# Transposing the operands of attention by DMA rather than on TensorE, in a fused attention and mixture kernel

## Chip, cores, metric

One core of a Trainium2 chip. The metric is the time of one execution on the device in microseconds (us). Profiles are of one execution each. Their "span" runs from the first to the last instruction. Most executions of a kernel agree within some tenths of a per cent. A run is called slow when it is over 1.5% above the fastest of the same kernel.

Engine names in the profile: PE is TensorE (PEld its weight loads), DVE is VectorE, ACT is ScalarE, POOL is GpSimd, SP the engine that here only issues DMAs.

## The reference, cut

```python
# attention: batch 4, 8 heads, 768 steps, head dimension 48
f = 1.0 / (1.0 + np.exp(-f_logit))
for t in range(S):
    state = f[:, :, t, :, None] * state + np.einsum('bhd,bhe->bhde', k[:, :, t], v[:, :, t])
    y[:, :, t] = np.einsum('bhd,bhde->bhe', q[:, :, t], state)
# mixture: 3072 tokens, d_model 384, d_ff 2048, x is y laid out by tokens
h = x @ w_in
P = a[0] + a[1] * h + a[2] * h * h + a[3] * h * h * h
Q = 1.0 + np.abs(b[0]) * np.abs(h) + np.abs(b[1]) * h * h
out = (P / (Q + 1e-06)) @ w_out
```

The work is cut into 12 units of 256 tokens (0 to 11). Attention of a unit runs chunk by chunk; its output is projected to 2048 columns in two groups of 8 x 256, on which P/Q is computed, and projected back.

## The kernel before

The order of all work is a fixed list of tokens, key and unit: `mq`/`mk` are the VectorE products that write q and k scaled (tile `qkp`), `T` transposes them, `Te` copies the result out of PSUM (tile `qkT`), `sc` are the scores that read it. In the mixture, `t` and `B` are two affine functions of y, `P` adds them, `U` adds |y| and its square, `O` copies out and stores.

```python
P_BY_DMA = {4, 5, 6, 7, 8, 9, 10, 11, 12, 13, 14, 15, 16, 17, 18, 19, 20, 21}
...
def a_T(n, ps=ALL):                                  # 16 blocks of 128x128 on PE
    ...
                nc.tensor.transpose(tp[:, b, i, p, :],
                                    s["qk"][:, i, ps.start + p, b].rearrange("t i d -> t (i d)"), ident)
def a_Te(n, ps=ALL):                                 # PSUM -> SBUF, on ACT or VectorE
    ...
        copy(te_engine(n), t.rearrange("p j a b c -> p (j a b c)"), ...)
...
def m_t(n):                                          # per group of 2048 columns
    nc.vector.tensor_scalar(tile_of(n, "t", bufs=3), mg[n]["y"], a_sb[:, 3:4], a_sb[:, 2:3],
                            op0=ALU.mult, op1=ALU.add)
def m_p(n):                                          # the last sum of the numerator
    if n in P_BY_DMA:
        nc.gpsimd.dma_start(out=s["t"], in_=s["pb"], accum_op=ALU.add)
    else:
        nc.vector.tensor_add(s["t"], s["t"], s["pb"])
...
def m_oe(m, b, eng, queue=None):
    osb = ms.tile([P, DM], F32, name="osb", bufs=4)
    copy(eng, osb, ops.pop((m, b)))
    ...
    (queue or nc.sync).dma_start(out=dst[:, b, :], in_=osb)        # stores: SP queue
...
# load(n): f, k and q of unit n, 384 KB each, also on the SP queue
```

Of the kernel before, what the change touches and what calls it, by code (L numbers as in the profile page):

```python
# [18 lines left out]
    efl-:0 efl:0 cs-:0 A0-:0 A1-:0 cs:0 A1:0 mk-:0 A0:0 mq-:0 T-:0 mk:0 mq:0 Te-:0 T:0 sc0:0 sv:0 Te:0  # L19
    efl:1 m0:0 al:0 sc1:0 st:0 cs:1 A0:1 m1:0 y-:0 mq:1 y:0 A1:1 mk:1 sw:0 su:0 xe:0 T:1 Te:1 ha0:0  # L20
    Ya0:0 ha1:0 sc0:1 sv:1 m0:1 Ya1:0 vl:3 al:1 st:1 sc1:1 za:0 efl:2 qa:0 cs:2 A1:2 ta:0 Ua:0 m1:1 sa:0
    hb0:0 sw:1 Ba:0 y:1 mk:2 A0:2 hb1:0 La0:0 Pa:0 Yb0:0 Ea:0 su:1 xe:1 mq:2 Yb1:0 T:2 ga:0 ha1:1 Te:2
    Ya1:1 ha0:1 zb:0 qb:0 Ya0:1 tb:0 Ub:0 Lb0:0 sc0:2 m0:2 Bb:0 hb0:1 sv:2 Ba:1 sc1:2 hb1:1 al:2 za:1
    m1:2 oa0:0 st:2 sw:2 Yb0:1 Eb:0 y:2 Yb1:1 qa:1 efl:3 sb:0 cs:3 xe:2 tb:1 A1:3 ta:1 Pb:0 ha1:2 A0:3
    zb:1 Ya1:2 gb:0 mq:3 ha0:2 Ya0:2 su:2 efl:4 qb:1 Bb:1 hb1:2 Yb1:2 oa1:0 Ua:1 Oa:0 cs:4 mk:3 T:3 Ub:1
    ta:2 La0:1 ob0:0 ob1:0 sa:1 sv:3 vl:4 Te:3 A1:4 sc0:3 qa:2 Ea:1 Ob:0 A0:4 efl:5 hb0:2 mk:4 m0:3
    sc1:3 mq:4 al:3 vl:5 m1:3 cs:5 st:3 sw:3 Lb0:1 sb:1 A0:5 y:3 za:2 Yb0:2 Pb:1 ua1:2 A1:5 qb:2 xe:3
    Eb:1 ua0:2 La1:2 su:3 T:4 sv:4 Pa:1 zb:2 La0:2 ga:1 Ub:2 ha0:3 Te:4 Ba:2 al:4 ha1:3 sc0:4 tb:2 mk:5
    gb:1 m0:4 Ya0:3 sa:2 efl:6 st:4 mq:5 vl:6 oa0:1 Bb:2 Ya1:3 Ea:2 oa1:1 sc1:4 hb1:3 sb:2 m1:4 sw:4
    Yb1:3 hb0:3 Oa:1 cs:6 Yb0:3 ob0:1 A0:6 y:4 za:3 qb:3 Pa:2 A1:6 ob1:1 qa:3 Lb0:2 ta:3 xe:4 su:4 T:5  # L30
    ha0:4 sa:3 zb:3 sv:5 Pb:2 Ba:3 ha1:4 ga:2 tb:3 Eb:2 Bb:3 Te:5 Ob:1 sc0:5 oa0:2 Ya0:4 efl:7 Ua:3 gb:2
    m0:5 mq:6 Ub:3 al:5 Pa:3 st:5 Ya1:4 oa1:2 Oa:2 hb0:4 sc1:5 La0:3 mk:6 Yb0:4 ob0:2 Ea:3 sw:5 sb:3
    vl:7 m1:5 hb1:4 ta:4 Yb1:4 cs:7 Lb0:3 qa:4 za:4 y:5 Ua:4 ob1:2 Ba:4 xe:5 T:6 sa:4 qb:4 zb:4 A1:7
    ha1:5 A0:7 su:5 sv:6 mq:7 Te:6 sc0:6 Pb:3 Ya1:5 Ob:2 ga:3 m0:6 Ub:4 ha0:5 sc1:6 al:6 st:6 Eb:3 oa0:3
    La0:4 hb0:5 Ya0:5 tb:4 m1:6 y:6 Ea:4 Pa:4 vl:8 sb:4 Bb:4 gb:3 za:5 sw:6 xe:6 mk:7 qa:5 oa1:3 Yb0:5
    Oa:3 hb1:5 ta:5 su:6 Ba:5 sa:5 T:7 Te:7 sv:7 ha1:6 efl:8 Yb1:5 ga:4 al:7 Lb0:4 Ya1:6 tb:5 cs:8 A0:8
    sc0:7 ob0:3 st:7 ob1:3 m0:7 zb:5 A1:8 ua1:5 sc1:7 Pb:4 sw:7 qb:5 m1:7 Eb:4 La1:5 ha0:6 gb:4 Ya0:6
    ua0:5 Ob:3 y:7 hb1:6 mq:8 efl:9 Bb:5 sb:5 mk:8 La0:5 xe:7 Pa:5 cs:9 Yb1:6 A0:9 T:8 Ub:5 ta:6 za:6
    oa0:4 Ea:5 Ba:6 qa:6 su:7 hb0:6 oa1:4 Te:8 A1:9 Yb0:6 ha1:7 sa:6 Lb0:5 ga:5 vl:9 ha0:7 Ya1:7 Oa:4
    sc0:8 Pb:5 tb:6 zb:6 sv:8 qb:6 ob0:4 m0:8 Pa:6 ua1:6 Ya0:7 al:8 Eb:5 mk:9 ua0:6 La1:6 st:8 La0:6  # L40
    sc1:8 ob1:4 sb:6 Bb:6 m1:8 Ba:7 za:7 sv:9 Ub:6 efl:10 hb0:7 Ea:6 y:8 hb1:7 Yb0:7 xe:8 gb:5 mq:9 Pb:6
    ha0:8 vl:10 Ob:4 qa:7 al:9 T:9 ta:7 Ua:7 Yb1:7 st:9 Bb:7 Lb0:6 ha1:8 Ya0:8 oa0:5 qb:7 Ya1:8 Te:9
    zb:7 oa1:5 Eb:6 Oa:5 cs:10 efl:11 ga:6 A0:10 A1:10 sa:7 sc0:9 Pa:7 hb0:8 tb:7 ob0:5 m0:9 sc1:9 gb:6
    ta:8 Yb0:8 mq:10 m1:9 ob1:5 hb1:8 La0:7 ub1:7 Ba:8 mk:10 qa:8 Yb1:8 y:9 Ob:5 za:8 Ea:7 Lb1:7 sb:7
    xe:9 vl:11 ga:7 ub0:7 tb:8 Lb0:7 Ua:8 zb:8 oa0:6 qb:8 cs:11 A1:11 T:10 A0:11 Pb:7 Te:10 Eb:7 Ub:8
    oa1:6 ha1:9 Oa:6 sa:8 sv:10 sc0:10 al:10 ha0:9 La0:8 st:10 mk:11 m0:10 Ya1:9 ob0:6 Ya0:9 Ea:8 ob1:6
    sc1:10 Pa:8 Lb0:8 sb:8 hb1:9 Bb:8 Ob:6 m1:10 hb0:9 Yb0:9 za:9 qa:9 sv:11 y:10 gb:7 ta:9 Yb1:9 xe:10
    mq:11 Ba:9 Eb:8 oa0:7 qb:9 Pb:8 al:11 T:11 Ua:9 zb:9 sa:9 Te:11 oa1:7 ga:8 ha0:10 Oa:7 sc0:11 tb:9
    La0:9 Ub:9 ha1:10 st:11 ob0:7 m0:11 sc1:11 Ya1:10 Ya0:10 Pa:9 Bb:9 ob1:7 Ea:9 sb:9 m1:11 hb0:10 Ob:7
    Lb0:9 hb1:10 za:10 qa:10 y:11 gb:8 Pb:9 Ua:10 Yb0:10 oa0:8 oa1:8 ta:10 Yb1:10 Ba:10 xe:11 Eb:9 Oa:8  # L50
    La0:10 sa:10 ha0:11 ha1:11 zb:10 qb:10 ob0:8 ga:9 Pa:10 Ub:10 tb:10 ob1:8 Bb:10 Ya0:11 sb:10 Ya1:11
    Pb:10 Ea:10 gb:9 za:11 hb1:11 Ob:8 Yb1:11 hb0:11 qa:11 Yb0:11 ta:11 Ba:11 oa0:9 sa:11 Ua:11 Lb0:10
    oa1:9 qb:11 zb:11 Oa:9 ob0:9 ga:10 tb:11 Ub:11 Eb:10 La0:11 ob1:9 Ea:11 Pa:11 Ob:9 gb:10 Lb0:11
    ob0:10 oa0:10 sb:11 Bb:11 ob1:10 Eb:11 ga:11 oa1:10 Oa:10 oa0:11 Pb:11 ob0:11 gb:11 ob1:11 oa1:11
    Oa:11 Ob:10 Ob:11
# [3 lines left out]
P_BY_DMA = {4, 5, 6, 7, 8, 9, 10, 11, 12, 13, 14, 15, 16, 17, 18, 19, 20, 21}  # L59

U_BY_DMA = {2, 3, 5, 6, 7, 8, 9, 11, 13, 14, 16, 17, 18, 19, 20, 21, 22, 23}

TE_ON_ACT = {1, 2, 4, 5, 6, 11}
O_ON_DVE = {(0, 1), (11, 1), (10, 1), (2, 0), (9, 1)}
# [3 lines left out]
def kernel(  # L68
# [12 lines left out]
    nc = tc.nc  # L81
# [61 lines left out]
    hold = w_pool.tile([1, 4, 16], BF16, name="hold")  # L143
# [6 lines left out]
    NUN = len(units)  # L150
    at_ = {}
# [3 lines left out]
    def load(n):  # L155
        c, u = units[n]
        at_[n] = dict(qk=qkp[n % NQK], ls=lsp[n % NQK], st=states[u], c=c, u=u)
        for name, src in (("fn", f_logit), ("kn", k), ("qn", q)):
            at_[n][name] = ld.tile([C, H, UB, D], F32, name=name)
            if n > 0:  # L160
                nc.sync.dma_start(out=at_[n][name].rearrange("p h b d -> p h (b d)"), in_=rows(src, n))
        if n == 0:
            for ps in HALVES:
                for name, src in (("fn", f_logit), ("kn", k), ("qn", q)):
                    for i in range(2):
                        hs = slice(HP * i + ps.start, HP * i + ps.stop)
                        nc.sync.dma_start(out=at_[n][name][:, hs].rearrange("t h b d -> t h (b d)"),
                                          in_=rows(src, n)[:, hs])

    def load_v(n):  # L170
        at_[n]["vn"] = vz[n % NV]
        for cc in range(UB):
            w = slice(CH * cc, CH * cc + CH)
            nc.gpsimd.dma_start(out=vz[n % NV][w, :, cc].rearrange("p h b d -> p h (b d)"), in_=rows(v, n)[w])  # L174

# [59 lines left out]
    def a_T(n, ps=ALL):  # L235

        s = at_[n]
        pool, tag = (psr, "r") if ps is HALVES[1] else (psA, "A")
        tp = pool.tile([P, UB, 2, npairs(ps), C], BF16, name="tp", tag=tag)
        for b in range(UB):  # L240
            for i in range(2):
                for p in range(npairs(ps)):
                    nc.tensor.transpose(tp[:, b, i, p, :],  # L243
                                        s["qk"][:, i, ps.start + p, b].rearrange("t i d -> t (i d)"),
                                        ident)
        s["tp", ps.start] = tp

# [3 lines left out]
    def a_Te(n, ps=ALL):  # L251
        s = at_[n]
        t = tile_at(s, "qkT", [P, UB, 2, HP, C], BF16)
        if ps is ALL:
            copy(te_engine(n), t.rearrange("p j a b c -> p (j a b c)"),
                 s["tp", 0].rearrange("p j a b c -> p (j a b c)"))
        else:
            copy(te_engine(n), t[:, :, :, ps].rearrange("p j a b c -> p (j a) (b c)"),
                 s["tp", ps.start].rearrange("p j a b c -> p (j a) (b c)"))
# [29 lines left out]
    def a_sc(n, half):  # L289
# [3 lines left out]
        for q_ in range(2):  # L293
            p = half * 2 + q_
            for b in range(UB):
                for i in range(2):
                    for cc in range(UB):
                        r, w = slice(64 * i, 64 * i + D), slice(CH * cc, CH * cc + CH)
                        nc.tensor.matmul(sc[w, i, q_, b, :], s["qkT"][r, b, 1, p, w], qcols(s, r, p, w),  # L299
# [7 lines left out]
    def qcols(s, r, p, w):  # L307
        return s["qkT"][r, :, 0, p, w]
# [10 lines left out]
    def a_y(n, ps=ALL):  # L319
# [7 lines left out]
        def clear(kk, r):  # L327
# [28 lines left out]
        if ps.start == 0:  # L356
            for kk in (0, KD - 1):
                clear(kk, slice(0, P))
        product(True, [(1, 1)])
        product(False, [(1, 1)])  # L360
        for i in range(2):
            if ps.start == 0:
                clear(0, slice(64 * i + 32, 64 * i + 48))
            if ps.stop == HP:
                clear(KD - 1, slice(64 * i, 64 * i + 16))
# [46 lines left out]

    def m_y(n, half):
        nc.scalar.copy(part_of(tile_of(n, "y"), half), mg[n]["hp", half].rearrange("p a n -> p (a n)"))  # L414

    def m_sq(n):
        s = mg[n]
        s["h2"] = ms.tile([P, W], BF16, name="h2")
        nc.vector.tensor_mul(s["h2"], s["y"], s["y"])  # L419

    def m_abs(n):
        s = mg[n]
        s["z"] = ms.tile([P, W], BF16, name="z")
        nc.vector.tensor_scalar(s["z"].bitcast(U16), s["y"].bitcast(U16), 0x7FFF, None,  # L424
# [21 lines left out]
    def m_ln(n, half):  # L446
        s = mg[n]
        lq = tile_of(n, "lq", F32, bufs=1)
        whole = "u" in s
        nc.scalar.activation(lq if whole else part_of(lq, half),  # L450
                             s["u"] if whole else s["u", half].rearrange("p a n -> p (a n)"),
                             AF.Ln, scale=sig[:, 2:3], bias=1.0 + 1e-6)
# [5 lines left out]

    def m_t(n):
        nc.vector.tensor_scalar(tile_of(n, "t", bufs=3), mg[n]["y"], a_sb[:, 3:4], a_sb[:, 2:3],  # L460
# [210 lines left out]
```

## Time and profile before

| | before |
|---|---|
| time, median of the first 3 runs | 234.65 us (233.94 to 234.94) |
| span of the profiled execution | 231.3 us |
| busy: PE, VectorE, ACT | 211.0, 212.1, 202.1 us |
| PE's waits ahead of the scores | 1.9 us in all |
| first absolute value (z) of the mixture | 27.15 us |
| accumulating DMAs of 512 KB | 36 |

From 27.15 us (the first z) to 223.64 us (its last product) VectorE is busy for 194.4 of 196.5 us. What the transposition costs is 16 blocks on PE and one copy (1.13 us on VectorE, 1.87 on ACT) for each unit.

### The profile page before, as it was taken

How to read it: one execution, taken by the hardware profiler on the slowest of the kernel's cores; microseconds unless marked ns; L12 is line 12 of the kernel's file. 1: busy time of each engine (PE TensorE's matmuls, PEld its weight loads, DVE VectorE, ACT ScalarE, POOL GpSimd, SP SyncE). 2: the span in 40 equal slices, each digit the busy share in tenths (PEclk: the TensorE clock that was granted, in tenths of full speed). 3: DMA queues.
4: the chain of work that ended last, by engine and by line, in shares of the span. 5: the costliest groups of instructions: out<-in, count | busy, mean ns of one | idle time of the engine just before them, and what ended most of it. 6: DMA issues, size and time to landing. Idle time of an engine off the chain costs nothing.

```text
span 231.3 us, 7110 instructions
## 1 busy us (share of the span) xinstructions
PE 211.0 (91%) x3106; PEld 150.1 (65%) x3106; DVE 212.1 (92%) x257; ACT 202.1 (87%) x202; POOL 66.3 (29%) x91
## 2 busy tenths in 40 slices
PE   7299797979989999999999999999999999997981
PEld 3166565767657767676776775876677878764540
DVE  5686599999999999999999999999999999999950
ACT  4424889997999999999999999999998999799950
POOL 8360860023305126035112411424132122313000
PEclk9959979999979999999999999999999999999998
DMA  7999999999999999999999999876599969998502
GB/s 108 261 144 202 186 188 199 222 250 258 197 272 262 187 222 206 183 272 194 185 202 247 192 261 203 131 140 125 74 181 212 203 120 205 188 213 198 127 34 102
DMA packets 63054, 43.71 MB, mean 189 GB/s; under 512 B 51760, under 2 KB 58416, under 8 KB 63024
## 3 DMA queue, kind: packets, MB, share of 16 engines
q0 software_dynamic: 21632, 24.38, 65.9%
q1 hardware_dynamic: 41104, 18.88, 32.7%
q8 instruction: 24, 0.39, 0.7%
q10 hardware_dynamic: 288, 0.00, 0.1%
q14 instruction: 6, 0.05, 0.1%
HBM read 25.17 MB, written 4.72 MB: 129 GB/s over the span
## 4 chain that ended last, share of the span: by engine, by line
DVE 58%; PE 21%; issue 10%; DMA 6%; ACT 3%; SPq 1%; POOL 0%; DVEq 0%; POOLq 0%; ACTq 0%
DVE scm L315 8%; DVE h L419 8%; DVE gall L485 8%; DVE t L465 7%; PE op L502 7%; PE hp L400 6%; DVE t L460 5%; DVE qkp L232 5%; DVE pb L468 5%; DVE z L424 4%; DVE qkT L249 2%; PE y L352 2%; DMA z<-h 2%; DVE t L476 2%; DVE state L381 2%
## 5 line engine op out<-in xcount | busy, mean ns | idle before, releaser
L400 PE MATMUL hp<-xT,w_in_sb 128*128 128x256 bf16 x576 | 70.2, 275 | 0.6 <-ACT y L414 0.2
L502 PE MATMUL op<-w_out_sb,gall 128*128 128x384 bf16 x368 | 65.5, 326 | 2.4 <-ACT osb L249 1.7
L400 PEld LDWEIGHTS <-w_in_sb 128*128 128x128 bf16 x576 | 55.1, 99 | 11.1 <-issue 2.0
L502 PEld LDWEIGHTS <-gall 128*128 128x128 bf16 x384 | 36.1, 98 | 26.4 <-issue 2.2
L414 ACT CAST y<-hp 128x1024 bf16<-128x1024 f32 x48 | 48.0, 1024 | 1.7 <-PE hp L400 0.9
L455 ACT ACTIVATE qi<-lq 128x2048 bf16<-128x2048 f32 x24 | 46.4, 1934 | 0.1
L450 ACT ACTIVATE lq<-z,sig 128x2048 f32<-128x2048 bf16 x20 | 40.4, 2020 | 2.9 <-DMA z<-h 2.8
L442 POOL DMA_DIRECT2D z<-h x18 | 17.1, 949 | 88.5 <-DVE z L424 38.4
L315 DVE TENSOR_TENSOR scm<-sc,mask 128x1024 bf16<-128x1024 f32 x24 | 29.1, 1213 | 4.2 <-PE sc L299 4.2
L474 POOL DMA_DIRECT2D t<-pb x18 | 17.5, 975 | 45.7 <-DVE t L465 30.1
L485 DVE TENSOR_TENSOR gall<-t,qi 128x2048 bf16<-128x2048 bf16 x24 | 29.1, 1211 | 1.0 <-ACT qi L455 1.0
L465 DVE TENSOR_TENSOR t<-t,h 128x2048 bf16<-128x2048 bf16 x24 | 29.1, 1211 | 0.0
L419 DVE TENSOR_TENSOR h<-y 128x2048 bf16<-128x2048 bf16 x24 | 29.0, 1211 | 0.0
L226 ACT ACTIVATE A<-cs 128x768 f32<-128x768 f32 (+1 forms) x26 | 18.7, 767 | 4.2 <-PE cs L217 4.1
L174 POOL DMA_DIRECT2D vz<-in_v_dram x24 | 21.8, 1131 | 0.3 <-POOL vz L531 0.3
L460 DVE TENSOR_SCALAR t<-y,a_sb 128x2048 bf16<-128x2048 bf16 x24 | 19.4, 811 | 0.5
L468 DVE TENSOR_SCALAR pb<-y,a_sb 128x2048 bf16<-128x2048 bf16 x24 | 19.4, 811 | 0.0
L424 DVE TENSOR_SCALAR z<-y 128x2048 uint16<-128x2048 uint16 x24 | 16.5, 688 | 0.5 <-ACT lq L450 0.4
L217 PE MATMUL cs<-lsp,U 128*128 128x384 bf16 (+1 forms) x39 | 10.9, 341 | 6.2 <-ACT lsp L204 6.1
L243 PE MATMUL tp<-ident,qkp 128*128 128x128 bf16 x192 | 13.8, 227 | 2.6 <-DVE qkp L232 2.4
L243 PEld LDWEIGHTS <-qkp 128*128 128x128 bf16 x192 | 12.2, 101 | 5.5 <-DVE qkp L232 3.5
L352 PE MATMUL y<-scm,vz 128*32 128x128 bf16 (+1 forms) x768 | 15.4, 228 | 0.0
(75 smaller groups left out, 253.7 us busy)
## 6 DMA issues: line engine op xcount, KB each, us to landing
z<-h POOLq DMA_DIRECT2D x18, 512.0 KB, 6.2
t<-pb POOLq DMA_DIRECT2D x18, 512.0 KB, 6.6
out_dram<-osb SPq DMA_DIRECT2D x24, 192.0 KB, 4.1
fn<-in_f_logit_dram SPq DMA_DIRECT2D x11, 384.0 KB, 5.9
kn<-in_k_dram SPq DMA_DIRECT2D x11, 384.0 KB, 6.1
qn<-in_q_dram SPq DMA_DIRECT2D x11, 384.0 KB, 6.9
vz<-in_v_dram POOLq DMA_DIRECT2D x24, 96.0 KB, 6.4
w_in_sb<-in_moe_w_in_dram POOLq DMA_DIRECT2D x8, 192.0 KB, 5.1
```

The costliest lines, as they stand in the source:

```text
L243: nc.tensor.transpose(tp[:, b, i, p, :], s["qk"][:, i, ps.start + p, b].rearrange("t i d -> t (i d)"), ident)
L315: nc.vector.tensor_mul(m.rearrange("s i q b t -> s (i q) (b t)"), s["sc", half].rearrange("s i q b t -> s (i q) (b t)"), mb)
L400: nc.tensor.matmul(hp[:, e, :], w_in_sb[:, kk, f * P:(f + 1) * P], xT[:, kk, :], start=(kk == 0), stop=(kk == KD - 1))
L414: nc.scalar.copy(part_of(tile_of(n, "y"), half), mg[n]["hp", half].rearrange("p a n -> p (a n)"))
L419: nc.vector.tensor_mul(s["h2"], s["y"], s["y"])
L450: nc.scalar.activation(lq if whole else part_of(lq, half), s["u"] if whole else s["u", half].rearrange("p a n -> p (a n)"), AF.Ln, scale=s ...
L455: nc.scalar.activation(part_of(tile_of(n, "qi"), part, parts), part_of(mg[n]["lq"], part, parts), AF.Exp, scale=-1.0)
L460: nc.vector.tensor_scalar(tile_of(n, "t", bufs=3), mg[n]["y"], a_sb[:, 3:4], a_sb[:, 2:3], op0=ALU.mult, op1=ALU.add)
L465: nc.vector.tensor_mul(s["t"], s["t"], s["h2"])
L468: nc.vector.tensor_scalar(tile_of(n, "pb"), mg[n]["y"], a_sb[:, 1:2], a_sb[:, 0:1], op0=ALU.mult, op1=ALU.add)
L485: nc.vector.tensor_mul(galls[m][:, lo:lo + w, :].rearrange("p a n -> p (a n)"), part_of(s["t"], part, parts), part_of(s["qi"], part, parts))
L502: nc.tensor.matmul(ops[m, b], galls[m][:, mm, b * C:(b + 1) * C], w_out_sb[:, mm, :], start=(mm == 0), stop=(mm == KF - 1))
```

## The change

Its intent: from unit 3 on the operands are transposed by one DMA from SBUF to SBUF, so PE loses the transposes and VectorE and ACT the copies. With the time freed, seven sums that had gone by accumulating DMA are computed on VectorE again; the two affines of a unit's two groups are merged into one instruction each, in place of y for `B`; the first loads are spread over three queues with f first; the last group is handled in halves; the order of work is laid out anew. The core of the diff:

```diff
-P_BY_DMA = {4, 5, ..., 21}                       # 18 groups
+P_BY_DMA = {3, 6, 7, 12, 13, 14, 15, 17, 18, 19, 21}
+    FIRST_BY_DMA = 3
 def a_T(n, ps=ALL):
+        if n >= FIRST_BY_DMA:
+            nc.sync.dma_start(out=qkT(s).rearrange("f i p b t -> f (i p b) t"),
+                              in_=s["qk"].rearrange("t i p b h d -> t (i p b h d)"), transpose=True)
+            return
+    steps["t2"] = lambda n: affine(both(n, "t"), both(n, "y"), 2)      # 4096 wide
+    steps["B2"] = lambda n: affine(both(n, "y"), both(n, "y"), 0)
 ... first loads:
+                        (nc.gpsimd if name == "qn" else nc.scalar if act else nc.sync).dma_start(
 ... later loads: behind the transpose, no longer behind the third reading
-            if read[n] == 3 and n + 3 < NUN:
-                load(n + 3)
+        if key == "T" and n + 3 < NUN:
+            load(n + 3)
 (the order of work, the lists for other engines, the start and the last group's halves: cut)
```

## The prediction

> **What bounds the kernel now.** I read the busy shares and the forty slices first. In the slices each digit is a tenth of busy time and a slice is 231.3/40 = 5.8 us.
>
> ```profile
> span 231.3 us, 7110 instructions
> PE 211.0 (91%) x3106; PEld 150.1 (65%) x3106; DVE 212.1 (92%) x257; ACT 202.1 (87%) x202; POOL 66.3 (29%) x91
> PE   7299797979989999999999999999999999997981
> DVE  5686599999999999999999999999999999999950
> ACT  4424889997999999999999999999998999799950
> DMA  7999999999999999999999999876599969998502
> ```
>
> Three engines are near full and nothing is slack in the middle. The holes are at the two ends: VectorE has 5, 6, 8, 6, 5 in the first five slices and 5, 0 in the last two. Next the table of stretches shows which engine is really shut (columns: stretch, PE, PEld, DVE, ACT and POOL busy with instruction counts, clock, DMA share, GB/s):
>
> ```profile
> 38.00:60.00 22.00, 20.54 (x284) 15.45 (x282) 22.00 (x27) 20.54 (x21) 5.44 (x6) 1.00 1.14 233
> 60.00:100.00 40.00, 38.24 (x605) 27.84 (x607) 39.96 (x47) 39.80 (x41) 9.09 (x10) 0.96 1.18 224
> 100.00:150.00 50.00, 49.49 (x889) 36.45 (x878) 49.78 (x58) 49.28 (x52) 15.49 (x17) 1.00 1.07 206
> ```
>
> VectorE is busy 22.00 of 22.00, 39.96 of 40 and 49.78 of 50 us, and 58% of the chain that ended last lies on it. So from 27 us (the first product of the mixture part) to 223.6 us (its last) VectorE's own work sets the time; PE and ACT follow by a few per cent. Taking work from PE or ACT alone buys little there. The timeline gives the real price of a VectorE instruction: starts, not durations, since neighbours overlap by about 0.08 us (columns: start, duration).
>
> ```profile
> 193.42 0.68 DVE L424 TENSOR_SCALAR z<-y 128x2048 uint16<-128x2048 uint16 x1
> 194.02 1.22 DVE L419 TENSOR_TENSOR h<-y 128x2048 bf16<-128x2048 bf16 x1
> 195.15 1.21 DVE L485 TENSOR_TENSOR gall<-t,qi 128x2048 bf16<-128x2048 bf16 x1
> 196.40 0.81 DVE L460 TENSOR_SCALAR t<-y,a_sb 128x2048 bf16<-128x2048 bf16 x1
> 197.13 0.81 DVE L468 TENSOR_SCALAR pb<-y,a_sb 128x2048 bf16<-128x2048 bf16 x1
> 197.85 1.22 DVE L465 TENSOR_TENSOR t<-t,h 128x2048 bf16<-128x2048 bf16 x1
> ```
>
> From start to start: a 2048-wide product costs 1.13, z 0.60, t or pb 0.72 us.
>
> **What the Trainium skill says.** (1) "DMA: Bandwidth & Descriptors", section "DMA Transpose (X-bar)": a plain DMA transpose is issued from the SP or ACT queue only and moves 2-byte data into SBUF; section "Latency and other measured facts" measures 261 GB/s for it. The trace before has no transposing DMA, so it neither agrees nor differs. (2) "VectorE: DVE Perf Modes", "The three transpose paths": 128x128 takes 390 ns on TensorE and 1309 ns by DMA. Here PE did 16 of them in 0.90 us from start to start (183.96 to 184.86), far below 16 x 390, because they are pipelined; whether sixteen by DMA pipeline is the open question. (3) Same page, "Mode 4×_2P": four bf16 per cycle when only one tensor is read; at 0.96 GHz 2048 elements would be 533 ns. z's 0.60 us agrees, t's 0.72 leaves about 0.19 us of fixed cost. (4) "DMA: Bandwidth & Descriptors", "Issuing engines are not separate DMA queues": spreading issues over engines saves only issue time. At the start that is just what is short: the twelve first loads are issued one by one, about 0.49 us each.
>
> **The change part by part.** I counted instructions of both programs per engine.
>
> VectorE, steady part. Removed: 5 copies of transposed operands, 5 x 1.13 = 5.65. Merged: 40 of the 48 affine instructions become 20 twice as long, saving one fixed cost each, 20 x 0.19 = 3.8. Output copies 5 to 3: 2 x 0.47 = 0.9. Added: the last sum of the numerator is now on VectorE for 13 groups and not 6 (the list handed to DMA shrinks from 18 to 11): 7 x 1.13 = 7.9. Net 5.65 + 3.8 + 0.9 - 7.9 = 2.4 us less. So most of what the transpose frees on the bounding engine is spent again on sums taken back from the DMA.
>
> ACT: 4 copies of 1.87 go (7.5 us), two output copies come (0.8); about 6.7 less. PE: 144 transposes go, 9 x 0.90 = 8.1; two more groups add h2 and |y| on PE, 16 more matmuls of 9.9/32 = 0.31 us each, 5.0; about 3 less. Both were not the bound, so this is slack and not time.
>
> DMA: 36 accumulating transfers of 512 KB become 27, and 9 transposes of 512 KB come. Bytes are equal. From the queue shares, the 18.9 MB of accumulates out of 24.4 MB on the software queue cost about 0.51 x 231.3/36 = 3.3 us of all 16 engines each (estimate); a transpose at the skill's 261 GB/s would cost 2.0 (estimate). So DMA gets no worse.
>
> Start. These lines show it before:
>
> ```profile
> 3.94 0.88 SPq L167 DMA_DIRECT2D fn<-in_f_logit_dram  x2
> 8.45 0.52 ACT L203 ACTIVATE ef<-fn 128x384 f32<-128x384 f32 x1 [3.02 <-DMA fn<-in_f_logit_dram]
> 11.73 0.55 DVE L232 TENSOR_TENSOR qkp<-qn,A 128x384 bf16<-128x384 f32 x1
> 22.76 1.87 ACT L249 COPY qkT<-tp 128x2048 bf16<-128x2048 bf16 x1 [1.14 <-PE tp L243]
> 27.15 0.70 DVE L424 TENSOR_SCALAR z<-y 128x2048 uint16<-128x2048 uint16 x1
> ```
>
> The second half of f is issued at 3.94, behind k and q, and read at 8.45. Now all of f is issued by about 1.7 (SP three, ACT one), which at the same 3.6 us to landing makes it ready near 5.8. But q goes to the GpSimd queue behind the building of the masks (1.8 us of GpSimd work, from 0.73), four issues of 0.79 us each, so to about 5.7, landing four later: the last q product can run near 9.8 instead of 11.73. So the gain at the first scores is about 1.8 us and not 2.7. Two more things shorten the way to the first z: the transposes of unit 1 (1.0 us on PE at 21.67) and their copy (1.87 us on ACT at 22.76, of which about 0.8 held up the first cast) now stand behind unit 0's projection in program order. Sum 3.6: the first z at about 23.5. The 3.5 us of clearing moved from GpSimd to VectorE lies in its idle time before that. One mask product that stood ahead of z now stands behind it: +1.1.
>
> End. Before:
>
> ```profile
> 218.42 2.02 ACT lq L450
> 220.46 1.92 ACT qi L455
> 222.40 1.24 DVE gall L485
> 223.68 2.79 PE op L502 x16
> ```
>
> Behind the last exponential (ends 222.37) come 8.9 us to the end of the span. Now the last group goes in halves: 0.7 for half a product, 8 matmuls 1.4, one copy 0.5, the store's 3.8 as before: 6.4. Gain 2.5.
>
> Sum: 231.3 - 3.6 - 2.4 + 1.1 - 2.5 = 223.9 us of span if nothing new waits. The timed median is 234.65 - 231.3 = 3.35 above the span: 227.3. I add 1.0 for new waits: **228.3 us**.
>
> **The new waits and the rivals.** What decides is whether a transpose lands in time. Between the last product that feeds it and the scores that read it, the changed program leaves PE other work of (units 3 to 11, summed from start-to-start costs: a projection half or output half 1.31, cumulative sums 1.3, y 1.95) 6.0, 7.4, 7.2, 11.5, 12.0, 10.7, 10.6, 13.6, 13.4 us. Alone a transpose should take about 4 (2.0 for the bytes, and 2 to 3 as the smallest loads show, 3.0 us). But its queue also holds the loads of the next units, three of 384 KB at 6 to 7 us to landing, and for unit 4 the transpose follows just behind such a set. So units 3 to 5 may wait one to three us each, later ones should not.
>
> Rival A, the transpose becomes the wait: if sixteen blocks went one by one at 1.3 us, 21 us each, every one of 9 units would wait some 8 us, and the time would be 250 to 300. For it: the DMA is busy throughout, nothing in this trace shows a transpose. Against it: the order of work leaves 6 to 13 us, as one would who had seen it land in less. A milder form, 10 to 12 us to landing, costs units 3 to 5 some 4 us each: 233 to 238.
>
> Rival B, the bound stays and the middle gains nothing: VectorE's 2.4 us are lost to coarser steps (a 4096-wide affine must wait for both halves of a unit) and only start and end count: 227.3 + 2.4 + 1 = about 230.5, within 2%. For it: VectorE was already waiting just 1.8 us in 196.
>
> Rival C, everything flows: three engines are relieved, ACT's waits for z<-h (2.8 us) shrink with fewer accumulates and no wait comes: 224 to 226.
>
> Rival D, the start is limited elsewhere: v and q now both come by the GpSimd queue, the second set of k and q waits for the first weights; the 3.6 us shrink to 1.5: about 230.
>
> **Range and chances.** My sum and C lie under 229.96, the border of 2%; B and D lie just over it; A far above. Weights: sum or C 0.65, B, D and mild mixtures 0.30, A 0.05. Range 223 to 233.
>
> **What would show it right or wrong.** Right: first z near 23.5 us; VectorE's 2048-wide affine rows replaced by 4096-wide ones near 1.26 us start to start; VectorE busy about 208; transposes landing under 8 us, and less than 3 us of PE waits on them; less than 7 us after the last exponential. Wrong: PE or VectorE idle before scores with a transpose named as releaser in every unit; first z at 25 or later; accumulates landing later than before (6.2 and 6.6 us); more VectorE idle than 5 us between the first z and the last product.

## The result

The changed kernel took **274.22 us** (median of 4 runs, 271.94 to 277.93) where the kernel before took 234.3 in the same rounds. The ratio is 1.169, 95% interval 1.157 to 1.180. Ratios here are the mean time of one kernel's fast runs over that of the other's fast runs of the same rounds, so not quite the ratio of the medians that I quote. The prediction was 228.3, and its range ended at 233.

The page of the changed kernel (busy times, then tenths in forty slices, now of 6.8 us each):

```profile
span 272.1 us, 6870 instructions
PE 214.0 (79%) x2988; PEld 147.5 (54%) x2988; DVE 211.5 (78%) x239; ACT 197.7 (73%) x204; POOL 63.0 (23%) x81
PE   7783989788179995089998099999829839998994
DVE  5786599999468996078999529999854857898991
```

Busy times have hardly moved, and the span is 40.8 us longer: this is idle time, and it lies in holes (1, 0, 0, 2, 3 on PE) that PE and VectorE share (ACT's row has them too). Hardly anything does more work; the engines wait, and for the same thing. In the table of stretches (as in the prediction) one of the three stretches is:

```profile
60.00:100.00 40.00, 31.20 (x518) 22.84 (x517) 33.00 (x36) 30.99 (x33) 7.58 (x8) 0.91 0.99 190
```

VectorE, once busy 39.96 of 40 us, is at 33.00; from 100 to 150 it has 37.95 us, before 49.78. PE's clock (the third number from the end) has fallen as well, from 0.96 to 0.91, and its own work became dearer: the same matmul of the projection (`hp`) takes 293 ns in the mean, before 275. So PE has 144 fewer transposes, 16 more adding matmuls and is still busy 214.0 us, before 211.0. The lists of waits name the releaser (columns: us in all, times, longest), here of PE, VectorE and ACT:

```profile
PE sc L320 <- DMA qkT<-qkp: 37.0, 6, 10.8
DVE scm L336 <- PE sc L320: 32.2, 8, 11.1
ACT y L447 <- PE hp L421: 38.5, 14, 9.7
```

PE stood 37.0 us before the scores until a transposed operand landed; VectorE and ACT then waited for PE. Issue and landing of unit 6 show why, in the timelines of SP, VectorE and PE (start, duration):

```profile
92.97 10.62 SPq L542 DMA_DIRECT2D out_dram<-osb  x2
96.38 0.95 DVE L243 TENSOR_TENSOR qkp<-qn,A 128x768 bf16<-128x768 f32 x1
103.68 5.88 SPq L251 DMA_TRANSPOSE qkT<-qkp  x1
116.84 0.64 PE L320 MATMUL sc<-qkT 48*64 48x128 bf16 x16 [10.85 <-DMA qkT<-qkp]
```

The same transpose from issue to landing, in the chain that ended last:

```profile
103.68 13.11 DMA qkT<-qkp
```

The operand was complete at 97.33. SP issues in order, and was held by two output stores until 103.6; a store waits for a copy of its result on ACT or VectorE. Then the transpose took 13.11 us from issue to landing. So 6.3 us of the lateness come before the issue and the rest after it. For the six units that PE waited for (3, 4, 6, 8, 10, 11) the issue came 0.1, 3.0, 6.3, 6.3, 11.3 and 16.0 us after the product: in unit 3 at once, in unit 4 behind three loads, in the other four behind stores. Unit 5 was issued 1.9 us late, behind stores as well, but PE hardly waited for it. Over the nine transposes the time to landing was 4.3 us at least, 8.8 in the median and 13.1 at most. Two theories follow. **Queue**: what stands ahead in SP's queue makes the transposes late. **Flight**: they share the DMA engines with the 512 KB accumulates and take 9 to 13 us in place of 4.

### The profile page after: what moved, and what is told of

Its sections match the earlier page's. It is cut to its first block, busy times and chain, and to the rows that moved or that the text cites. A ratio compares the mean times of both kernels' runs of the same rounds, so it can differ in the third digit from the quotient of the medians.

```text
span 272.1 us, 6870 instructions
## 1 busy us (share of the span) xinstructions
PE 214.0 (79%) x2988; PEld 147.5 (54%) x2988; DVE 211.5 (78%) x239; ACT 197.7 (73%) x204; POOL 63.0 (23%) x81
## 4 chain that ended last, share of the span: by engine, by line
PE 34%; DMA 31%; DVE 19%; ACT 6%; issue 6%; POOL 2%; SPq 0%; ACTq 0%; POOLq 0%; DVEq 0%
DMA qkT<-qkp 19%; PE hp L421 15%; PE op L533 10%; DMA t<-y 7%; PE y L373 3%; DMA fn<-in_f_logit_dram 3%; DVE h L452 3%; DVE scm L336 3%; DMA w_in_sb<-in_moe_w_in_dram 3%; DVE qkp L243 3%; PE sc L320 2%; DVE t L498 2%; ACT y L447 2%; DVE t L492 2%; PE u L467 1%
## 5 line engine op out<-in xcount | busy, mean ns | idle before, releaser
L487 ACT ACTIVATE qi<-lq 128x2048 bf16<-128x2048 f32 (+1 forms) x25 | 46.2, 1852 | 0.1
L320 PE MATMUL sc<-qkT 48*64 48x128 bf16 x384 | 11.6, 248 | 37.4 <-DMA qkT<-qkp 37.0
L484 ACT ACTIVATE lq<-z,sig 128x2048 f32<-128x2048 bf16 (+1 forms) x19 | 36.5, 1925 | 0.6 <-DMA z<-h 0.5
L516 DVE TENSOR_TENSOR gall<-t,qi 128x2048 bf16<-128x2048 bf16 (+1 forms) x25 | 29.2, 1175 | 6.6 <-ACT y L447 5.1
L320 PEld LDWEIGHTS <-qkT 48*64 48x64 bf16 x384 | 7.3, 120 | 43.8 <-DMA qkT<-qkp 39.6
L270 ACT COPY osb<-op 128x384 f32<-128x384 f32 x21 | 10.1, 481 | 13.5 <-PE op L533 13.5
L492 DVE TENSOR_SCALAR y<-y,a_sb 128x4096 bf16<-128x4096 bf16 (+1 forms) x14 | 16.8, 1202 | 0.2
L492 DVE TENSOR_SCALAR t<-y,a_sb 128x4096 bf16<-128x4096 bf16 (+1 forms) x14 | 16.6, 1188 | 0.2
L507 DVE TENSOR_TENSOR t<-t,y 128x2048 bf16<-128x2048 bf16 x13 | 15.7, 1218 | 0.1
L505 POOL DMA_DIRECT2D t<-y x11 | 10.2, 950 | 20.2 <-DVE t L498 8.8
```

The lines of the kernel that those rows point to most:

```text
L320: nc.tensor.matmul(sc[w, i, q_, b, :], qkT(s)[r, 1, p, b, w], qcols(s, r, p, w), start=True, stop=True)
L484: nc.scalar.activation(lq if whole else part_of(lq, half), u, AF.Ln, scale=sig[:, 2:3], bias=1.0 + 1e-6)
L487: nc.scalar.activation(part_of(tile_of(n, "qi"), part, parts), part_of(mg[n]["lq"], part, parts), AF.Exp, scale=-1.0)
L492: nc.vector.tensor_scalar(out, y, a_sb[:, c + 1:c + 2], a_sb[:, c:c + 1], op0=ALU.mult, op1=ALU.add)
L516: nc.vector.tensor_mul(galls[m][:, lo:lo + w, :].rearrange("p a n -> p (a n)"), part_of(one(n, "t"), part, parts), part_of(s["qi"], part, ...
```

## The experiments

Ratios are to the kernel before, run in the same rounds (232.7 to 233.4 us; 234.3 for the changed kernel). A median is that of all runs, a ratio that of the fast ones alone.

| kernel | median us | ratio, fast runs |
|---|---|---|
| changed | 274.22 | 1.169 |
| r1: changed, stores behind the transposes | 248.29 (one fast run, 244.02) | |
| r2: before, only the DMA transposes added | 272.16 | 1.168 |
| r3: changed, all transposes on PE | 247.37 | 1.061 |
| r4: before, start of the change | 238.2 | 1.023 |
| r6 / r7: r1 / r3 with another load order | 250.37 / 250.81 | 1.073 / 1.075 |
| r8: r10, early loads by need | 236.51 | 1.012 |
| r9: r1, loads of units 2 and 3 exchanged | 245.6 | 1.050 |
| r10: r4 with the halved tail | 237.34 | 1.017 |
| r11: r9 with three buffers | 244.05 | 1.048 |
| r12: r1, accumulates held | 258.37 | 1.108 |
| r13: r3, 18 sums by DMA | 256.33 | 1.098 |
| r14: r2, stores behind | 288.11 (fast: 280.17, 284.14) | 1.209 |
| r15: r11, 18 sums by DMA | 269.59 (one fast run, 249.44) | |
| r16: before, 11 sums by DMA | 240.52 | 1.027 |
| r17 / r18: r3 / r13 with three buffers | 245.55 / 250.73 | 1.050 / 1.073 |

r5 measures flights and is not compared. All results were correct.

### The queue: stores behind the transposes (r1)

```diff
-        osb = ms.tile([P, DM], F32, name="osb", bufs=4)
+        osb = ms.tile([P, DM], F32, name="osb", bufs=6)
-        (queue or nc.sync).dma_start(out=dst[:, b, :], in_=osb)
+        late.append((dst[:, b, :], osb))      # issued just behind the next transpose
+        if key == "T":
+            flush()
```

> The output stores that stood ahead of a transpose in the SP queue are issued behind it instead; nothing else changes. Theory 'queue': five of the nine transposes are late because SP, which works in order, holds them behind stores whose output copy is not done (issue 1.9, 6.3, 6.3, 11.3 and 16.0 us after the last product that feeds them). Taking this lateness off the 37.0 us that PE waits for transposes leaves about 11 us, so about 274 - 26 = 248 us. Theory 'flight': what counts is the 9 to 13 us between issue and landing; then units 3 to 6 still wait 4 to 5 us each, new waits appear where the earlier issue meets more traffic, PE waits stay above 25 us and the time above 262.

Measured: 244.0 to 250.8 us, three of four runs slow, so no exact size; all are over 20 us below the changed kernel. (The granted clock of the slow ones, 0.938 to 0.972, lies on both sides of the fast one's 0.954.) PE's waits for transposes fell from 37.0 to 11.2 us (profile of a slow run). The same queue after one further exchange of loads, r9, has a profile, and there one sees the queue turn round. SP's own waits, first of the changed kernel:

```profile
SPq L542 <- ACT osb L270: 107.9, 18, 14.6
SPq L251 <- DVE qkp L243: 6.4, 3, 5.5
```

and of r9, with PE's wait for transposes:

```profile
SPq L551 <- ACT osb L270: 49.4, 11, 11.3
SPq L251 <- DVE qkp L243: 49.2, 8, 10.3
PE sc L320 <- DMA qkT<-qkp: 7.3, 1, 7.3
```

In the changed kernel SP stood at stores for 107.9 us, and for the product of a transpose (L251) for 6.4: when its turn came, the operand was mostly there. In r9 SP stands at the transpose and waits for the product, 49.2 us. Of the two sides "queue" is the one that came: its 248 us lie within the four runs.

### The transposes alone (r2)

```diff
 # kernel before, its order, its lists, its start
+        if n >= 3:
+            nc.sync.dma_start(out=qkT(s)..., in_=s["qk"]..., transpose=True)
+            return
 # and load(n + 3) stands behind T:n
```

> The kernel before with its own order of work; only the transposes from unit 3 on go by DMA (and a unit's loads are issued behind its transpose). If the transposes by themselves are the cause, this is far slower than 234: its order leaves only 2 to 6 us between products and scores, so each of nine units waits 4 to 10 us: 270 to 310. If it is the changed order or the start that costs the time, this stays within 234 to 245.

Measured: 272.16 us, ratio 1.168 (1.161 to 1.175). The landing took 9.4 us in the median, and PE's waits have the same line at their head:

```profile
PE sc L311 <- DMA qkT<-qkp: 33.5, 7, 11.2
```

The DMA transposes alone, with the loads behind them, are enough for the whole slowdown. (No run moves those loads alone; in r2's lists the waits for loads are as before, ACT's for f 5.3 us and before 5.4.) This does not make the other parts free, as r3 shows.

### The reverse: all transposes on PE (r3)

```diff
-    FIRST_BY_DMA = 3
+    FIRST_BY_DMA = 99
-        pool, tag = (psr, "r") if ps is HALVES[1] else (psA, "A")
+        pool, tag = (psr, "r") if ps is HALVES[1] or n > 2 else (psA, "A")
 # and T, Te of units 3 to 11 a few steps ahead of their scores
```

> The changed kernel with every transpose on PE again (into the two rotating PSUM buffers, copied by ACT for units 3, 5, 6, 10 and VectorE for the other five), set some five places ahead of the scores; all else of the change stays. If the DMA transposes are the whole cause: 226 to 234 us, PE waiting less than 5 us in the middle. If the merged affines, the start or the new order cost much themselves: above 240.

Measured: 247.37 us, ratio 1.061. Some 27 us go, but not 40: a miss of the expectation that nothing else costs. VectorE was busy 216.7 of 244.9 us, so idle for 28. Each part is thus bad by itself, and their costs do not add: while PE waits for a transpose, other delays lie hidden beside it.

### The price of one flight (r5)

```diff
 # appended to the kernel before
+    tr(sA, 0); hold_until(sA)                 # alone, full size; then full, half, one eighth
+    tr(sA, 1); hold_until(sA)
+    tr(sA, 0, 8); hold_until(sA)
+    tr(sA, 1, 2); hold_until(sA)
+    load f, k, q (384 KB each); tr(sB, 0)     # behind three loads
+    tr(sA, 0)                                 # beside two accumulates of 512 KB
+    for x in acc: nc.gpsimd.dma_start(out=x, in_=sB, accum_op=ALU.add)
```

> The kernel before with transposes appended when all its work is done: full size alone (twice, the first beside the last stores), half and an eighth of it alone, full behind three loads of 384 KB on the same queue, full beside two accumulating transfers of 512 KB, and two accumulates alone. Result stays correct, time about 40 to 60 us longer. Theory 'flight by sharing': alone 4 to 5 us, SP busy under 2 us; behind loads 8 to 11; beside accumulates 8 to 13. Rival 'the transpose is slow in itself': alone 8 us or more, and half size near half. Rival 'only late issue': behind loads and beside accumulates under 6 us as well.

Measured, as pieces of the chain (start, duration). In order: 16 blocks alone, 8, 2, 16 behind three loads, 16 beside two accumulates.

```profile
233.34 4.29 DMA sA<-qkp
239.30 3.05 DMA sA<-qkp
244.04 2.33 DMA sA<-qkp
249.21 6.12 DMA sB<-qkp
255.99 12.60 DMA sA<-qkp
```

From 2 to 16 blocks 1.96 us are added: 0.14 us a block. So sixteen blocks do pipeline, and alone the flight is 4.3 us, as I had estimated. Loads ahead add 1.8. Beside accumulates it is three times as long. Of the last case, the rate in forty slices and the two queues (packets, MB, share of 16 engines):

```profile
GB/s 0 0 0 0 0 199 160 185 210 198 185 133 197 209 80 237 241 220 195 154 151 193 203 158 119 106 119 145 99 141 85 75 86 56 75 65 47 15 12 12
q0 software_dynamic: 287, 1.05, 50.2%
q1 hardware_dynamic: 2112, 0.52, 24.1%
```

The transpose moves 0.52 MB in 2112 packets of some 250 bytes, the accumulates 1.05 MB in 287 of some 3.7 KB. The Trainium skill ("DMA: Bandwidth & Descriptors", section "Queues, rings and completion order") says that each DMA engine takes turns between its queues packet by packet. With such packets, if they are what the page means by the word, turns favour the accumulates some fifteenfold in bytes (an estimate from these counts). The long flight agrees with that; the turns themselves can be seen in a stretch of r14 below. A second thing is in the rates: they sink from about 200 to 12 GB/s at the end, some sixteenth of the full rate, so the last pieces seem to lie on very few engines. The same page ("Latency and other measured facts") has engines 7 and 15 usually slower in traces, with a guess at the descriptors of GpSimd's DMAs as the cause; which engine was last, the profile here does not tell.

### Queue or flight, in the order of the kernel before (r14)

The edit of r1, applied to r2, with one difference: here the stores stand between the transpose and the next unit's loads, in r1 behind both.

> The kernel before with nothing but the DMA transposes from unit 3 on (272.2 us, PE waited 33.5 us for them), and now the output stores issued behind the next transpose. 'Queue': most of the lateness was stores ahead of a transpose in the SP queue, as in the changed kernel: PE's waits for transposes fall to about 10 us and the time to 244 to 250 us. 'Flight': the 36 accumulates of the kernel before share the engines with the transposes, so flights stay at 9 to 14 us, PE's waits stay above 20 us, and the time stays above 256 us.

Measured: the two fast runs took 280.17 and 284.14 us. That is slower than r2, and "queue" fails. In the profile (280.17 us, fast) the waits of SP and PE:

```profile
SPq L240 <- DVE qkp L232: 66.8, 9, 15.1
PE sc L311 <- DMA qkT<-qkp: 42.6, 5, 14.9
```

a piece of the chain:

```profile
105.30 24.35 DMA qkT<-qkp
```

and the DMA rates in forty slices over those 24.35 us:

```profile
GB/s 209 221 214 192 196 184 186 191 188 198 309 277 79 32 259 294 81 35 77 42 15 14 14 34 89 14 14 14 7 15 21 34 75 122 222 219 235 196 219 260
```

SP now stands at the transposes, nine of nine, before the product is there, so no store makes one late. Yet one of them took 24.35 us, and PE waited 42.6 us in all. Four accumulates were issued within the first ten us of it. From the middle on, nine of eleven slices show 7 to 21 GB/s, about a sixteenth of the rate at the start: for some 7 us the DMA moved about what one engine moves, and the transpose still had not landed. The DMA queues in the middle of that stretch, from 120.6 to 123.8 us:

```profile
q0 software_dynamic: 11, 0.04, 6.4%
q1 hardware_dynamic: 11, 0.00, 0.6%
```

In 3.2 us 11 packets of the accumulates' queue began (3.7 KB in the mean) and 11 of SP's (of 256 bytes in the trace, the size of a transpose's), in strict alternation, and the first fill 6.4% of sixteen engines' time, that is one engine's. So here the turns of the skill's page are seen: each small piece of the transpose stands behind a large one of an accumulate. The other engines were not free either: over 117 to 124 us 43 accumulate packets fill 95.0% of sixteen engines' time, some 2.5 us each (worked out) where those 11 took 0.3. What they waited for is not shown.

So early issue repairs the changed kernel, with 27 accumulates, and does nothing here, with 36 of them and an order of work that, in this stretch at least, puts them beside the transpose. Whether their number or their place counts, these two runs do not tell. Both theories are needed.

### Accumulates held until the transpose has landed (r12)

```diff
 # on top of r1
+        if key == "T" and n >= FIRST_BY_DMA:
+            nc.gpsimd.tensor_copy(hold[0:1, 0, :], at_[n]["qkT"][0:1, 1, HP - 1, UB - 1, 0:16])
```

> As r1, and GpSimd, which issues the accumulating transfers, first waits at each transpose's place in its order until that transpose has landed, so that accumulates issued later do not share the engines with it. Theory 'flight by sharing': the transposes' flights fall from 4 to 13 (median 5.6 in r1) to 4 to 7, none over 8 unless it meets older accumulates, and PE's waits for them from 11.2 to under 6 us. The time need not fall, since accumulates are held back: 244 to 252. Rival 'not the accumulates': flights over 8 us stay.

Measured: 258.37 us, ratio 1.108; slower than r1. The median flight fell from 5.6 to 4.5 us, as "flight" says. Three stayed long: 9.8 us in unit 4, right behind a set of loads; 15.2 in unit 5, issued at 77.20, just behind three accumulates of 72.6 to 75.6 that the hold had let go; and 23.2 in unit 10, beside six accumulates, three of them issued during the flight, since the hold stands behind them in GpSimd's order. So the hold kept only some accumulates off, and PE still waited 11.0 us. The accumulates now came late themselves, as ACT's and VectorE's waits show:

```profile
ACT y L447 <- DMA t<-y: 21.6, 5, 7.5
DVE h L452 <- DMA z<-h: 15.9, 2, 10.5
```

The collision cannot simply be pushed to the other side: both transfers have readers with little slack.

### What is left over without the transposes' waits

**The start (r4).** The change's start on the kernel before; unit 3's loads stand behind unit 2's.

```diff
-                for name, src in (("fn", f_logit), ("kn", k), ("qn", q)):      # for each half, all on SP
+                (nc.gpsimd if name == "qn" else nc.scalar if act else nc.sync).dma_start(...)
 # clearing moved to VectorE, v and the second unit's loads in the change's places
```

> The kernel before with only the start of the change: unit 0's loads spread over three queues with f first, the clearing moved to VectorE, unit 0's steps in the new order, unit 3's loads kept behind those of unit 2. If the start is worth what the first z suggests (21.2 us and not 27.2, of which the second half of the weights takes some back): 227 to 231 us. If the early z only waits later for weights and v: 231 to 234. If the start as such is harmful: above 236.

Measured: 238.2 us, ratio 1.023 (1.015 to 1.030): slower, though the interval reaches below 2%. The first z came at 20.73 us rather than 27.15, and was no use. ACT stood 6.41 us for f of unit 2 (to 30.06), and VectorE was busy 25.60 us between 27 and 60, before 33.00. So the start as changed costs some 5 us here: the first unit hurries and the third has no data.

**With the halved tail (r10).** `Eb-`, `gb-`, `oa1-`, `ob1-`: exponential, product and output of the last group in halves.

> As r4, and the last group of the last unit in halves and quarters as in the change (logarithm, exponential, product, output). Expected 2 to 2.5 us below r4: the stretch behind the last exponential falls from 8.9 to about 6.4 us. This is the candidate to beat both kernels: 225 to 229. If the end is held by VectorE or the DMA instead: equal to r4 within 1 us.

Measured: 237.34 us, ratio 1.017, about 1 us under r4, which is within the noise of the two, and not the 2.5 that I had counted. In its chain PE runs 28 output matmuls from 225.78 to 230.52 us, past the end of the halved last product (229.33), and four more after a copy: the end of the kernel had gone from VectorE to PE.

**Early loads in order of need (r8).** v of unit 1, the second half of the weights and unit 2's loads moved ahead, to behind `Te:0`.

> As r10 (the kernel before with start and tail of the change), with the early loads in the order in which they are needed: v of unit 1 and the second half of the first weights go out as soon as the first half has, without waiting for k of unit 1, and unit 2's loads are not held behind them. In r4 ACT waited 6.4 us for f of unit 2, held behind those weights, and VectorE 4.9 us after it. Theory 'order of the early loads': both go, 229 to 233 us, at or below the kernel before. Rival 'the DMA is full at the start, so any order loses somewhere': 235 to 238.

Measured: 236.51 us, ratio 1.012 (1.006 to 1.018). Still slower than before, by less than 2%. In its profile (a slow run) the wait had passed to k on VectorE, 5.4 us. This fits a start in which the DMA has no room to give: early bytes for one reader are late ones for the next.

**Load order in the changed kernel (r6, r7, r9).** r6 and r7 put unit 3's loads behind unit 2's in r1 and r3; r9 puts unit 2's where unit 3's stood.

```diff
 # r6, r7
+            load(3)                      # behind last_loads(), no longer behind T:0
-        if key == "T" and n + 3 < NUN:
+        if key == "T" and 0 < n < NUN - 3:
 # r9
-        load(2)                          # in last_loads()
+            load(3)
-            load(n + 3)
+            load(n + 3 if n else 2)
```

> As r1, and the loads of unit 3 no longer go ahead of the second half of the first weights, of v of unit 1 and of unit 2 (in the changed kernel they are issued at 14.9 to 20 us because the step that triggers them comes before the step that issues those). Theory 'start loads': the second half of those weights, landing at 27.9 us, and v of unit 1, at 25.1, come 3 to 6 us earlier, PE's waits of 2.6 and 1.6 us there go, and the time falls from 248 by 3 to 6 us, to 242 to 245. Rival 'the start is full': the DMA carries about 200 GB/s through the first 30 us whatever the order, or the gain is lost again in the middle: within 2 us of 248.

> As r3 (all transposes on PE), with the same change of the load order as r6. Theory 'start loads' explains part of why r3 was at 247 and not 230: 241 to 244. The rest, about 10 us, is then the order of work, which was drawn for a VectorE without 5 copies and a PE without 144 transposes, and VectorE's sums taken back from the DMA. Rival: the start costs nothing and it stays at 246 to 248.

> As r1 (stores behind the transposes), but unit 2's loads stand where the changed kernel has unit 3's, and unit 3's behind the holds. r6 moved unit 3's back alone and left unit 2's behind the second weights; that did not help. Theory 'order of the early loads': f of unit 2 is no longer late, 243 to 246 us. Rival 'lost again in the middle': 247 to 250 as r1 and r6.

Measured: 250.37 and 250.81 us, both misses (r7 is 3.4 us slower than r3): unit 2's loads still stood behind the hold on the second half of the weights, so nothing came earlier. r9: 245.6 us (fast runs 243.8 to 246.2), within its expectation, but r1 spreads over 7 us and the gain of one to three us is small against that.

**Three buffers for y and t (r11, r17).**

```diff
-            units_of[m, name] = ms.tile([P, NG * W], BF16, name=name)
+            units_of[m, name] = ms.tile([P, NG * W], BF16, name=name, bufs=3)
```

> As r9, with three instead of two buffers for the merged y and t. In r1 ACT waited 7.2 us in 4 waits with a transfer t<-y named: the change reads y itself in that transfer (before it had a copy of its own), so y is held until it lands. Theory 'held y': 3 to 6 us less than r9. Rival: the wait only moves to the next one in line (z<-h or the scores), within 1.5 us of r9.

> The changed kernel with all transposes on PE (247.4 us), with three buffers for the merged y and t in place of two. 'Held buffers': the merged affines hold y of a whole unit longer, casts wait for it, and a third buffer frees them: 240 to 244 us. 'Order of work': short waits of every kind remain, 245 to 249 us.

Measured: 244.05 us after 245.6, and 245.55 after 247.37: 1.5 to 1.8 us each, less than was asked (3 us and more), and in r11 within the spread of its runs (241.1 to 245.4). Merged y and t held too long are a small part.

**The sums taken back (r16, r13, r15, r18).** One line: the list `P_BY_DMA` of the one kernel in the other. r16 puts the list of 11 into the kernel before; r13 puts the list of 18 into r3, r15 into r11; r18 is r13 with three buffers.

> The kernel before with one list exchanged: the last sum goes by DMA for the changed kernel's 11 groups and not for 18, everything else as it was. 'Sums taken back': VectorE sets the time there, so 7 x 1.13 = 7.9 us are added: 239 to 242 us. 'Slack elsewhere': waits for the accumulates that go away pay for it, and the time stays at 232 to 236 us.

Measured: 240.52 us, ratio 1.027 (1.021 to 1.033), VectorE busy 219.5 where it was 212.1: the seven sums cost their 7 us in full, and VectorE's slices are at 9 from the eighth on, as they were from the sixth on before.

> The changed kernel with all transposes on PE (247.4 us) and, in addition, the kernel before's list of 18 groups whose last sum goes by an accumulating DMA (the change had cut it to 11). 'Sums taken back': if VectorE's own work still sets the time there (it was busy 216.7 of 244.9 us), 7 sums of 1.13 us leave it, VectorE busy about 209, and the time comes to 237 to 241 us. 'Order of work': if the many short waits among PE, ACT and VectorE, from an order laid out for a kernel without these copies, set it, VectorE's busy time falls the same but the time stays at 245 to 250 us.

Measured: 256.33 us, 9 us *slower* than r3, though VectorE's busy time fell by 7.0 to 209.7. Handing the sums back to DMA in the new order made casts and products wait for their landing, though a landing took hardly longer (median 7.4 us, before 6.9): ACT's casts waited 9.1 us in five waits, in r3 2.8 in two, and VectorE itself stood 6.6 us before a product for the same. Neither theory had this. A busy time that falls is worth nothing where its reader comes sooner than the transfer can.

> The changed kernel with all transposes on PE and 18 sums by DMA (256.3 us; casts waited 9.1 us for sums that had yet to land), with three buffers. 'Held buffers': those casts wait no longer, the 7.9 us off VectorE are then worth something, and the time is 238 to 246 us. 'Order of work': VectorE still waits for the landing of sums where it reads them, 251 to 257 us.

Measured: 250.73 us. A third buffer wins back 5.6 of the 9 us, and the waits of casts leave the head of ACT's list; one product still waits 7.0 us for a landing. Close to the "order of work" side.

> The changed kernel with stores behind the transposes, loads in order of units and three buffers for y and t (244.1 us), and the kernel before's list of 18 groups summed by DMA. 'Sums taken back': 7 sums of 1.13 us leave VectorE and the time falls to 236 to 241 us. 'Shared flights': seven more accumulates of 512 KB stand beside the transposes, PE's waits for them rise above the 6.5 us that they were, and the time stays at 243 to 252 us.

Measured: one fast run of 249.44, three slow ones of 268 to 271.5. The fast one is 5.4 us over r11, so "sums taken back" fails here too, and "shared flights" has its 243 to 252. The profile fell on a slow run (one transpose took 34.64 us in it), so I draw no size from it.

No version beat the kernel before.

## Why the prediction was wrong, by its own steps

**What bounds the kernel before: right.** r16 confirms it: 7.9 us of work computed for VectorE, some 7 us of time.

**The first z: right in direction, and earlier than said, but no gain.** Predicted 23.5, measured 21.16, against 27.15:

```profile
21.16 0.69 DVE L457 TENSOR_SCALAR z<-y 128x2048 uint16<-128x2048 uint16 x1
```

I took its shift for a shift of the whole. In the first 60 us VectorE did 49.1 us of work, before 49.5. PE stood 1.63 us for the second half of the weights at 27.88 and 2.59 us for v of unit 1 at 25.14. Rival D was the better reading in kind, though not in size, and r4 puts the start at about 5 us of loss in the order of the kernel before.

**Merged affines: right.** 1.26 us start to start predicted. The trace has 1.25 (a `t2` starts at 50.09, the next instruction at 51.34).

**VectorE busy: predicted 208, measured 211.5.** My own net of 2.4 us less gives 209.7, not 208. The clearing that moved to VectorE adds 3.5 us, which I had named in the start and left out of the busy sum; but the masks, which I left out too, went from eight copies to four, some 2.6 us less. So the clearing does not explain the difference alone. Another slip: I put the time 3.35 us above the span, from two different runs; the profiled run itself took 233.4 us, 2.1 above its span.

**The end: right in the changed kernel, with less worth.** From the last exponential (265.26) to the end of the span it took 6.8 us, predicted 6.4. In r10 the halved tail was worth about 1 us, as PE was then the one that ended.

**The step that failed** is "What decides is whether a transpose lands in time ... later ones should not". I set PE's 6 to 13.6 us of other work against a flight that began when the last product ended. Both terms of the landing, its start and its flight, were mis-sized. The issue was up to 16.0 us behind the product, since SP's order also carries stores that wait for copies on ACT; I had named the loads in that queue and forgotten the stores. And the flight had been estimated alone, at about 4 us (r5: 4.3, right), where among the kernel's other transfers it took 8.8 in the median and up to 13.1. The slack was there: the units with the most of it by my list, 10 and 11, were 11.3 and 16.0 us late in issue and still made PE wait 5.0 and 5.8 us. Waits predicted under 3 us, measured 37.0.

**Rival A** was the one that came, with 0.05. I had rejected its reason (blocks one by one; r5 shows they pipeline) and with it the outcome, which another reason brought about. Its milder form, 10 to 12 us to landing, had the flight about right (8.8 in the median, up to 13.1), but not the late issue, and so gave 233 to 238. "The order of work leaves 6 to 13 us, as one would who had seen it land in less" was an argument from the author's mind, not from the trace.

**What stays open.** Without the transposes' waits 11 to 14 us remain (244 to 247 against 233). The start (about 5 on the kernel before) and the sums taken back (about 7 on it) have that size together, but r13 and r15 show that handing the sums to DMA again does not return it in the new order. So the rest is a property of that order and its transfers as a whole, which single exchanges did not take apart. Nor is it shown why one engine lags so far behind the rest: r14's stretch shows how its pieces take turns with the accumulates', not why the others were held as well.

## What to carry to other kernels

Before work is moved to a DMA, ask when its issue comes up in its queue, not only how long it flies: list what stands ahead of it on that engine and what *those* wait for. Then size the flight beside the traffic that will really be there; alone it was 4.3 us, beside two accumulates 12.6. And work that is pipelined on an engine with some slack, as 0.90 us of PE and a copy here, can be cheaper than a transfer that needs 10 us of lead in an order of work that does not leave them.

## What the Trainium skill lacked or had wrong

- "VectorE: DVE Perf Modes", section "The three transpose paths": 1309 ns for one 128x128 block by DMA. Sixteen in one transfer took 4.29 us, two 2.33 us: 0.14 us a block on top of a fixed part of about 2. The page does not say that blocks of one transfer overlap.
- "DMA: Bandwidth & Descriptors", section "DMA Transpose (X-bar)": no word on how long a transpose takes beside accumulates of another queue; the page's rules speak of a transpose beside ordinary DMAs only as to wrong data. It took 12.6 us here beside two of 512 KB, and up to 24.35 us in r14.
- The same page, "Latency and other measured facts": 261 GB/s for a transpose, of one kernel whose middle dimension was not contiguous. From 2 to 16 blocks, 0.46 MB in 1.96 us are some 234 GB/s (worked out from r5), a little below.
- No page that I found has the measured time for which a transpose holds the issuing engine on trn2 (the same page has a count of sequencer cycles only for "previous generations", in a table on trn3): SP was busy 1.85 to 7.20 us with each in the changed kernel, and 1.18 to 1.78 with the ones alone in r5.
